# A fused forward and backward pass: spectra stores moved to SyncE, lag matrices made earlier, and a new order of transfers in the last stage

## The chip, the cores and the metric

The kernel runs on one core of a Trainium2 chip. The metric is the device time of one execution in microseconds. Before the change the median of three runs is 741.45 us (740.36 to 741.85). The core has five engines with an instruction order of their own: TensorE (PE: matrix products into PSUM), VectorE (DVE), ScalarE (ACT), GpSimd (POOL) and SyncE (SP, which here only issues transfers). SP, ScalarE and GpSimd can each issue DMA transfers; the issue is an instruction in that engine's order, so whatever stands behind it on that engine waits for it.

## The reference, cut to what matters

With L = 2048 rows, D = 512 channels, N = 128 states and F = 1792 hidden units, all inputs bf16:

```
xn  = layernorm(x)
K   = real(sum_n C * exp(dt*A*l) * dt*B)           # 512 x 2048, a state-space kernel
s   = causal_conv(xn, K) + xn * Dskip               # through a transform of length 2L
h   = xn @ w1;  f = silu(h) @ w2;  g = silu(f)
out = x + s * g
```

The function returns `out` and, for a given grad_out, the gradients of x, of the eight state-space parameters, of w1 (output 10, 512 x 1792) and of w2 (output 11): twelve outputs. The backward pass of the dense part needs dh = (df @ w2^T) * silu'(h), then dx += dh @ w1^T and dw1 = xn^T @ dh.

## The kernel before

The rows stand in 16 tiles of 128. The convolution is done with matrix products against tables of a transform that is split into four classes kt; U, D and K spectra (of xn, of the gradient and of the state-space kernel) are made class by class, multiplied on VectorE (`cplx_mul`), and turned back. Spectra and other large intermediates that do not fit into the on-chip memory go to DRAM and come back (`UXd`, `DXd`, `Kud`, `hTd`, `dhd`, `Sd`, `gd`). There are six stages, one function each, and the order of instructions on each engine is the order in which the Python code issues them: nothing is rescheduled. Generators (`prev`, `fin`, `gx` and so on) are advanced step by step to lay one part's work between the steps of another. Tiles come from pools on two stacks, `k.left` and `k.right`; where a pool is closed and another opened, the new tile lies over the old one, and its first writer waits for the old one's last reader, transfers included.

Each transfer signals one of eight completion semaphores, in turn; SP and ScalarE share one set of eight, in the program's order, and GpSimd has another. So an issue also waits until the transfer eight places earlier in that list has landed.

What the change and the prediction's steps touch:

- **End of stage 2** (`stage_2`, from about L1082). `load_K` (L885 on) brings the state-space kernel K back from DRAM in 17 pieces over all three queues (SP, ScalarE, GpSimd). Then come, on GpSimd's queue, one table (`TFs1`), one spectrum of another class (`UXl`), the store of spectrum `UXd[3]` (inside `radix(3)`) and the store of `DXd[3]` (L1099). `rad_inv` on VectorE writes the tile BK3 (L97, L98) in memory that overlaps the stored U spectrum; `dskip_out` and then the first step of K's transform (`add_eo`, L1174) follow it.
- **Stage 4** (the loop over t0 in steps of 2). At t0 == 10 `gsum_sel` (L1192) makes the lag matrices: 0/1 matrices that later sum parts of a gradient by lag group. It is a few index patterns on GpSimd and 15 short VectorE operations. Stage 5's weight-gradient products (L1595) run on TensorE beside it.
- **Out0** (L1344 on) makes output 0: it loads S, g and x tiles, multiplies and adds on VectorE, stores the result and issues the next three loads. In the last loop of stage 6 it runs at four of the sixteen steps, and its transfers are issued by ScalarE.
- **Stage 6, first loop** (n = 0 to 27). `B.dh(n)` (L1858) does silu'(h) on ScalarE (`sd`, L132), eight matmuls da (L1870), the product dhT on VectorE (L1871), then has SP load h for step n + 3 (`ld_h`, tile `hsb`, three buffers) and store the previous step's dhT (`flush`, L1879). For n < 7 one piece of W1 is loaded with a DMA transpose into W1T behind each step (L1950). From n = 7 on, a generator `B.dx` interleaves half a row tile of dx = dhT @ W1T (seven matmuls, L1893) with each step; it reads the first half of W1T in its first half and the second half in its second. `B.dot` transposes the next 512 rows of the gradient (L1849).
- **Stage 6, last loop** (16 steps of 16 matmuls, L1981). Four column chunks times four row blocks of output 10. For each of them ScalarE copies PSUM into `o10b` (three buffers, L1983). SP loads the chunks `dhc` with DMA transposes (L1946), two ahead of each of the first steps, and stores the o10b of the step before (L1993).

Of the kernel before, what the change touches and what calls it, by code (L numbers as in the profile page):

```python
# [1002 lines left out]
def stage_2(k):  # L1003

    nc = k.nc
    lo, ro = k.left, k.right
    k.tf2 = ro.open("tf2"); k.xs = ro.open("xs", 2); sb = ro.open("sb"); k.slot[1] = (sb, ro.open("cyb")); dsc = ro.open("dsc"); uw = ro.open("uw", 2)
    st = k.st = {}
    k.put = nc.sync.dma_start
    DskT = k.DskT = uw.tile([P, P], BF16, name="DskT", bufs=1)  # L1010
    nc.gpsimd.memset(DskT[:], 0.0)
    gw = gen_w2t(k, lo.open("w2s"))

    def rad(XU):
        t = k.mm.tile([P, 2, 4, W], BF16, name="r4_t", tag="cm_t2")[:].rearrange("p e (c m) w -> p e c m w", c=2)
        rad4(nc, XU[:, :, 0:2], XU[:, :, 2:4], XU, t, False)

    def radix(b, q=nc.gpsimd):
        XU = st[b]["A"]
        rad(XU)  # L1020
        q.dma_start(k.UXd[b], XU[:])

    def front(b):
        st[b] = {}
        TFs = st["TF"] = k.TFs
        k.TFs = ld_tf(k, (b + 1) % 4)
        return fwd_classes(k, uw, k.xn, TFs, st[b])
    for b in range(2):
        fr = front(b)
        if b == 0:  # L1030
            open_tables(k, 1, nc.sync)
            open_y(k, 1)
            ld_tab(k, 1)
            next(gw)
            for e in range(2):
                nc.sync.dma_start(DskT[65 * e:65 * e + 33:32], k.ins["Dskip"].rearrange("(s d) -> s d", d=P)[2 * e:2 * e + 2])
        for _ in fr:
            tables_0(k)
    for b in range(NB):
        Kg = chunk_K(k, b, k.tabs[b])  # L1040
        Tc, Tn = k.gc.get(b + 1), k.gt.get(b + 1)
        gx = gen_xt(k, k.xs, b)
        gy = [gen_yt(k, k.xs, i) for i in (4 * b, 4 * b + 2)]
        sl = [gx] * 11 + [g for g in gy for _ in range(2)]
        if b == 3:
            for _ in Kg:
                pass
            break
        if b == 2:
            sl, gy2 = sl[:11], sl[11:]  # L1050
        if b:
            open_y(k, b + 1)
        fr = front(b + 2) if b < 2 else fwd_classes(k, dsc, k.DS, st["TF"], st.setdefault("D", {}))
        for j in range(15):
            if j in ((3, 9), (0, 3, 6), (0, 3))[b]:
                next(gw)
            if j in ((8, 10, 12, 14), (1, 4, 7, 10), (8, 13))[b]:
                next(fr)
            if j < 4:
                next(Tc, None)  # L1060
            if j == 0 and b < 2:
                next(k.gt[b])
            if j == 4 and b < 2:
                ld_tab(k, b + 2)
            if j % 2 == 0:
                next(Kg, None)
            if j < len(sl):
                next(sl[j])
            if b == 0 and j in (1, 3):
                radix(j // 2)  # L1070
            if b == 2 and j == 3:
                radix(2)
            if j == 10 and b < 2:
                open_tables(k, b + 2, nc.sync)
            if j in (4, 6, 8, 10, 12, 14):
                next(Tn)
    store_K(k)
    next(k.gt[2])
    for g in gy2:
        next(g)  # L1080
    held = []
    k.put = lambda *a: held.append(a)  # L1082
    lo.close("w2s", "xc", "ko", "sa")
    k.do = lo.open("do")
    K_b = k.do.tile([P, T, D], BF16, name="K_b", tag="DO")
    for _ in fr:
        pass
    load_K(k, K_b)
    k.by = lo.open("by"); k.uxp = lo.open("uxl")
    k.TFs1 = ld_tf(k, 1, nc.gpsimd)  # L1090
    UX = ld_ux(k, 0)
    radix(3)
    next(k.gt[3])
    sl = iter(sl)
    for n in range(8):
        next(next(sl))
    XD = st["D"]["A"]
    rad(XD)
    nc.gpsimd.dma_start(k.DXd[3], XD[:])  # L1099
    PX = cplx_mul(nc, k.mm, st[3]["A"], XD, conj_a=True)  # L1100
    ro.close("uw", "dsc", "cyb")
    k.BY = k.by.tile([P, 4, 2, 4, W], BF16, name="BY", tag="B")
    k.tn = lo.open("tn"); bk3 = lo.open("bk3")
    kq = k.kq = lo.open("kq")
    k.sel = lo.open("sel")
    k.row = k.sel.tile([DK, P], BF16, name="row")
    psd = k.psd = k.ps.tile([P, DK, P], F32, name="ps_dsk", tag="pz", bufs=1)
    for kt in range(4):
        for t in range(T):
            nc.tensor.matmul(out=psd[:, kt], lhsT=k.DS[:, t, kt * P:(kt + 1) * P], rhs=k.xn[:, t, kt * P:(kt + 1) * P], start=(t == 0), stop=(t == T - 1))  # L1110
    gk = gen_kt(k, kq, K_b, UX)
    next(gk)
    k.BK3 = rad_inv(k, bk3, "BK3", PX)
    k.dskb = dskip_out(k)
    return gk, sl, held


# [226 lines left out]
class Out0:  # L1344
# [15 lines left out]
    def run(self, t0, pool=False):  # L1360
        k, (S, g, x) = self.k, self.ins.pop(t0)
        TT = k.nc.vector.tensor_tensor
        TT(out=S[:], in0=S[:], in1=g[:], op=ALU.mult)
        TT(out=S[:], in0=S[:], in1=x[:], op=ALU.add)
        q = k.nc.gpsimd if pool else k.nc.scalar
        q.dma_start(k.o0_v[:, t0:t0 + TS, :], S[:])
        self.load(t0 + 2 * TS, q)

# [46 lines left out]
def stage_4(k):  # L1415

    nc = k.nc
    lo, ro = k.left, k.right
    y = k.y
    k.TI = {}  # L1420
    k.bk = lo.open("bk")
    dx = DXform(k, k.bk, k.kq)
    for kt in range(2):
        for _ in dx.front(kt):
            pass
    dx.mul(0)
    dx.inv(0)
    for t0 in range(0, T, TS):
        if t0 == 4:
            dx.mul(1)  # L1430
            dx.inv(1)
        if t0 == 8:
            for _ in dx.front(2):
                pass
            dx.mul(2)
        if t0 >= 4:
            y.sil(t0)
            y.pre(t0)
        TI = y.TI.pop(t0)
        ps = k.pd.tile([P, TS, W], F32, name="ps_v", tag="pd")  # L1440
        inv_mm(k, ps, [k.BY[:, i] for i in range(4)], TI, t0, (0, 1, 2, 3))
        S_s = k.y2.tile([P, TS, W], BF16, name="S_s", tag="S_s")
        nc.scalar.activation(out=S_s[:], in_=ps[:], func=ACT.Copy, scale=1.0 / L)  # L1443
        if t0 + 6 < T:
            y.load_ti(t0 + 6)
        else:
            k.TI[t0 + 6 - T] = ld_ti(k, k.tip, t0 + 6 - T)
        o = y.out(t0, S_s)
        if 2 <= t0 < T - 4:
            y.load(t0 + 4)  # L1450
        nc.sync.dma_start(*o)
        if t0 == 6:
            store_rows(k, k.row, k.outs[9], k.dskb)
        if t0 == 10:
            dx.inv(2)
            k.sels = gsum_sel(k, k.sel)
            k.pr.mul(0)
            k.pr.load(1)
        if t0 + 4 == T:
            k.w2 = Dw2(k)  # L1460
    ro.close("y2")
# [372 lines left out]
class Bwd:  # L1834
# [23 lines left out]
    def dh(self, n):  # L1858
        k, nc = self.k, self.k.nc
# [10 lines left out]
                nc.tensor.matmul(out=ps[:, j], lhsT=self.W2T[:, ft // 2, dk, j * P:(j + 1) * P], rhs=self.DOT[tc_][:, dk], start=(dk == 0), stop=(dk == DK - 1))  # L1870
        nc.vector.tensor_tensor(out=self.dhT[:, f0:f0 + 2, :], in0=ps[:], in1=sd[:], op=ALU.mult)  # L1871
        if n + 3 < 28:
            self.ld_h(n + 3)
        self.flush()
        self.pend.append((k.dhd[tc_, f0 * P:(f0 + 2) * P].rearrange("(a p) t -> p a t", p=P), self.dhT[:, f0:f0 + 2, :]))

# [47 lines left out]
def stage_6(k):  # L1924
    nc = k.nc
    lo, ro = k.left, k.right
    fw = k.fw
    W1T = k.tfp.tile([P, FT, D], BF16, name="W1T", tag="W1")
# [13 lines left out]
    def ld_ch(i, tc_):  # L1942
# [2 lines left out]
            ch[i] = pool.tile([P, T, FC], BF16, name="dhc", tag=tag)  # L1945
        nc.sync.dma_start_transpose(ch[i][:, 4 * tc_:4 * tc_ + 4, :], k.dhd[tc_, FC * i:FC * i + FC])  # L1946
    for n in range(28):
        B.dh(n)
        if n < 7:
            nc.sync.dma_start_transpose(W1T[:, 2 * n:2 * n + 2], k.ins["w1"][:, 256 * n:256 * n + 256])  # L1950
        next(prev, None)
        if n == 8 or n >= 21:
            next(fin, None)
        if n in (22, 23, 24, 26):
            ld_ch(0, min(n - 22, 3))
        if n in (8, 9):
            z.load((n - 8) * TS, nc.sync)
        if n in (11, 14, 16, 18):
            z.run(TS * (11, 14, 16, 18).index(n), True)
        if n % 7 == 5 and n < 26:  # L1960
            B.dot(n // 7 + 1)
        if n % 7 == 6:
            for _ in prev:
                pass
            prev = B.dx(n // 7, B.dhT)
# [1 line left out]
    order = [(i, tc_) for i in (1, 2, 3) for tc_ in range(4)]  # L1967
    ld_ch(*order.pop(0))
    ld_ch(*order.pop(0))
    pend = []  # L1970
    at = (6, 8, 10, 12)
    next(prev)
    for i in range(4):
        for dk in range(DK):
# [6 lines left out]
                nc.tensor.matmul(out=ps[:], lhsT=k.xn[:, t, dk * P:(dk + 1) * P], rhs=ch[i][:, t, :], start=(t == 0), stop=(t == T - 1))  # L1981
            ob = ww.tile([P, FC], BF16, name="o10b", tag="o10b")
            nc.scalar.copy(out=ob[:], in_=ps[:])  # L1983
            next(prev, None)
            next(fin, None)
            it = DK * i + dk
# [2 lines left out]
            if i == 1 and dk == 0:  # L1989
                B.rest()  # L1990
                B.flush()
            if pend:
                nc.sync.dma_start(*pend.pop())  # L1993
            pend.append((o10v[:, dk, FC * i:FC * i + FC], ob[:]))
    assert next(fin, k) is k
    nc.sync.dma_start(*pend.pop())
    ro.close("fp4", "ww", "fx", "fw", "wt", "tip", "tf2", "tfp")
    lo.close("oz", "fb", "do", "mm", "ds")

# [29 lines left out]
```

## Time and profile before

| | |
|---|---|
| median of 3 runs | 741.45 us |
| the profiled execution: device time | 748.97 us |
| its span, first to last instruction | 747.2 us |
| mean granted TensorE clock | 0.957 |
| busy: TensorE | 659.1 us (88%) |
| busy: VectorE | 619.4 us (83%) |
| busy: ScalarE | 418.1 us (56%) |
| busy: GpSimd | 122.4 us (16%) |
| DRAM traffic | 253 GB/s over the span |

The profile is one execution, so every duration in it belongs to 748.97 us and not to the median. "Busy" counts an engine's instructions and not the DMA issues. Times in windows and timelines count from the first instruction. "Idle before" is the time in which an engine did nothing ahead of an instruction, and the arrow names what was released last; where it says "issue" the profile saw no releaser, which can be a transfer. The granted clock is the share of TensorE's full rate: at 0.5 a matmul takes twice as long.

### The profile page before, as it was taken

How to read it: one execution, taken by the hardware profiler on the slowest of the kernel's cores; microseconds unless marked ns; L12 is line 12 of the kernel's file. 1: busy time of each engine (PE TensorE's matmuls, PEld its weight loads, DVE VectorE, ACT ScalarE, POOL GpSimd, SP SyncE). 2: the span in 40 equal slices, each digit the busy share in tenths (PEclk: the TensorE clock that was granted, in tenths of full speed). 3: DMA queues.
4: the chain of work that ended last, by engine and by line, in shares of the span. 5: the costliest groups of instructions: out<-in, count | busy, mean ns of one | idle time of the engine just before them, and what ended most of it. 6: DMA issues, size and time to landing. Idle time of an engine off the chain costs nothing. (4 is left out here: it accounts for less than half of the span.)

```text
span 747.2 us, 13309 instructions
## 1 busy us (share of the span) xinstructions
PE 659.1 (88%) x5132; PEld 336.8 (45%) x5132; DVE 619.4 (83%) x965; ACT 418.1 (56%) x513; POOL 122.4 (16%) x184
## 2 busy tenths in 40 slices
PE   4778877799878777999999899999999979999988
PEld 2434444354545656554444344444444434444543
DVE  6799999989899799599999999944577549899570
ACT  4789888995568967365534322344656523443231
POOL 2334171021011002100001212041222002200000
PEclk9998998899999998999999999999999989999999
DMA  9647767889898978999767879799886997999992
GB/s 268 236 165 246 236 229 240 266 298 358 268 317 275 301 222 182 296 347 359 287 227 286 287 288 353 215 316 335 272 283 232 240 307 248 321 242 221 225 266 87
DMA packets 167361, 198.83 MB, mean 266 GB/s; under 512 B 58461, under 2 KB 128484, under 8 KB 161378
## 3 DMA queue, kind: packets, MB, share of 16 engines
q1 hardware_dynamic: 150882, 132.63, 58.1%
q0 software_dynamic: 11200, 51.98, 19.8%
q10 hardware_dynamic: 5216, 13.38, 5.4%
q8 instruction: 40, 0.66, 0.4%
q14 instruction: 23, 0.19, 0.1%
HBM read 105.38 MB, written 83.38 MB: 253 GB/s over the span
## 5 line engine op out<-in xcount | busy, mean ns | idle before, releaser
L607 PE MATMUL ps_h<-XNT,W 128*128 128x512 bf16 x224 | 60.8, 421 | 12.2 <-ACT hs L610 12.2
L1188 PEld LDWEIGHTS <-TIs 128*128 128x128 bf16 x384 | 37.7, 99 | 51.7 <-issue 4.9
L1893 PE MATMUL ps_dx<-W1T,dhT 128*128 128x512 bf16 x224 | 53.8, 384 | 5.5 <-DMA W1T<-in_B_w_dram 4.6
L580 PE MATMUL ps_o<-W,aT 128*128 128x512 bf16 x224 | 55.7, 399 | 2.5 <-DVE ak L76 2.5
L1870 PE MATMUL ps_da<-DOT,W2T 128*128 128x512 bf16 x224 | 53.9, 388 | 2.3 <-DVE dhT L1871 2.3
L1981 PE MATMUL ps_w<-dhc,xn 128*128 128x448 bf16 x256 | 51.3, 361 | 3.1 <-ACT o10b L1983 3.1
L1595 PE MATMUL ps_w<-DO_all,AW 128*128 128x512 bf16 x224 | 52.0, 380 | 0.0
L1871 DVE TENSOR_TENSOR dhT<-ps_da,sd 128x1024 bf16<-128x1024 f32 x28 | 34.1, 1222 | 18.9 <-ACT sd L132 14.0
L1902 ACT ACTIVATE dxn<-dxn,c,rstd 128x512 f32<-128x512 f32 x16 | 13.0, 814 | 65.6 <-DVE c L1901 65.6
L1781 DVE TENSOR_TENSOR T<-Vb,YTl 128x2048 bf16<-128x2048 bf16 x16 | 19.6, 1224 | 35.2 <-ACT Vb L1772 34.9
L1164 PEld LDWEIGHTS <-TFs 128*128 128x128 bf16 x312 | 30.1, 98 | 38.6 <-issue 2.1
L934 ACT COPY XT<-pt_xt 128x1024 bf16<-128x1024 bf16 (+1 forms) x44 | 41.4, 1009 | 5.2 <-DMA XTd<-XT 3.2
L1772 ACT CAST Vb<-ps_V 128x1024 bf16<-128x1024 f32 x32 | 31.7, 1013 | 16.8 <-PE ps_V L1770 11.5
L1164 PE MATMUL ps_f<-K_b,TFs 128*128 128x512 bf16 x168 | 39.1, 379 | 1.5 <-DMA K_b<-Kud 1.3
L607 PEld LDWEIGHTS <-W 128*128 128x128 bf16 x224 | 22.8, 106 | 38.3 <-issue 21.8
L1981 PEld LDWEIGHTS <-xn 128*128 128x128 bf16 x256 | 25.5, 100 | 28.1 <-issue 5.6
L580 PEld LDWEIGHTS <-aT 128*128 128x128 bf16 x224 | 22.9, 102 | 32.0 <-issue 8.3
L1893 PEld LDWEIGHTS <-dhT 128*128 128x128 bf16 x224 | 22.0, 99 | 33.3 <-issue 7.5
L1870 PEld LDWEIGHTS <-W2T 128*128 128x128 bf16 x224 | 22.0, 99 | 30.2 <-issue 6.4
L998 PE MATMUL ps_f<-xn,TFs 128*128 128x512 bf16 x128 | 32.7, 411 | 3.3 <-DMA TFs<-TFd 3.3
L1164 PE MATMUL ps_f<-DS,TFs 128*128 128x512 bf16 x144 | 33.0, 379 | 1.8 <-ACT S_s L1443 1.8
L932 PE MATMUL pt_xt<-ident_bfloat,X 128*128 128x128 bf16 x328 | 25.7, 228 | 8.9 <-ACT XT L934 6.9
(342 smaller groups left out, 1510.6 us busy)
## 6 DMA issues: line engine op xcount, KB each, us to landing
TIs<-TId SPq DMA_DIRECT2D x24, 512.0 KB, 6.6
XTd<-XT SPq DMA_DIRECT2D x20, 512.0 KB, 5.8
XTl<-XTd SPq DMA_DIRECT2D x15, 512.0 KB, 8.6
hTd<-hs SPq DMA_DIRECT2D x28, 256.0 KB, 3.5
akd<-ak SPq DMA_DIRECT2D x28, 256.0 KB, 3.3
UXl<-UXd POOLq DMA_DIRECT2D x7, 1024.0 KB, 7.7
dhd<-dhT SPq DMA_DIRECT2D x28, 256.0 KB, 4.2
XYd<-XYg SPq DMA_DIRECT2D x25, 256.0 KB, 4.0
```

Source lines behind the costliest of these rows:

```text
L580: nc.tensor.matmul(out=pso[:], lhsT=aT[:, ft, tt * P:(tt + 1) * P], rhs=W2[:, ft, :], start=(ft == 0), stop=(ft == FT - 1))
L607: nc.tensor.matmul(out=ps[:, j], lhsT=W1[:, dk, ft * P:(ft + 1) * P], rhs=XNT[:, dk], start=(dk == 0), stop=(dk == DK - 1))
L934: nc.scalar.copy(out=XT[:, j0:j0 + len(ks)], in_=pt[:, 0:len(ks)])
L998: nc.tensor.matmul(out=ps[:, c, :], lhsT=TFs[:, t1 + 4 * j, c, :], rhs=src[:, t1 + 4 * j, :], start=(j == 0), stop=(j == 3))
L1164: nc.tensor.matmul(out=ps[:, c, :], lhsT=tab(j), rhs=at(t1 + 4 * j), start=(n == 0), stop=(n == 4 * len(terms) - 1))
L1188: nc.tensor.matmul(out=ps[:, j, :], lhsT=TIs[:, j, 2 * kt + c, :], rhs=B[kt][:, c, (t0 + j) % 4, :], start=(kt == 0 and c == 0), stop=(kt ...
L1595: nc.tensor.matmul(out=ps[:], lhsT=A[:, t, :], rhs=k.DO[:, t, :], start=(t == 0), stop=(t == T - 1))
L1772: nc.scalar.copy(out=self.V[i][:, g2], in_=ps[:].rearrange("p b c n -> p c b n"))
L1870: nc.tensor.matmul(out=ps[:, j], lhsT=self.W2T[:, ft // 2, dk, j * P:(j + 1) * P], rhs=self.DOT[tc_][:, dk], start=(dk == 0), stop=(dk == ...
L1871: nc.vector.tensor_tensor(out=self.dhT[:, f0:f0 + 2, :], in0=ps[:], in1=sd[:], op=ALU.mult)
L1893: nc.tensor.matmul(out=psx[:], lhsT=dhT[:, ft, t % 4 * P:(t % 4 + 1) * P], rhs=self.W1T[:, ft, :], start=(ft == 0), stop=(ft == FT - 1))
L1981: nc.tensor.matmul(out=ps[:], lhsT=k.xn[:, t, dk * P:(dk + 1) * P], rhs=ch[i][:, t, :], start=(t == 0), stop=(t == T - 1))
```

## The change

Six edits. (1) The stores of UXd[3] and DXd[3] are issued by SP instead of GpSimd. (2) `gsum_sel` is called at the end of stage 2, behind `dskip_out`, instead of in stage 4. (3) Out0's transfers in the last loop are issued by SP instead of ScalarE, and it runs one step later. (4) The h loads issued in steps 0 to 6 are ScalarE's. (5) The W1T pieces are issued ahead of steps 0 to 5, two of them ahead of step 0, instead of behind steps 0 to 6. (6) Each o10b block is stored by ScalarE directly behind its copy instead of by SP one step later.

```diff
@@ stage_2
-    radix(3)
+    radix(3, nc.sync)
...
-    nc.gpsimd.dma_start(k.DXd[3], XD[:])
+    nc.sync.dma_start(k.DXd[3], XD[:])
...
     k.BK3 = rad_inv(k, bk3, "BK3", PX)
     k.dskb = dskip_out(k)
+    k.sels = gsum_sel(k, k.sel)
     return gk, sl, held
@@ Out0.run
-        q = k.nc.gpsimd if pool else k.nc.scalar
+        q = k.nc.gpsimd if pool else k.nc.sync
@@ stage 4, t0 == 10
             dx.inv(2)
-            k.sels = gsum_sel(k, k.sel)
             k.pr.mul(0)
             k.pr.load(1)
@@ dh
-            self.ld_h(n + 3)
+            self.ld_h(n + 3, nc.scalar if n < 7 else None)
@@ stage_6, first loop
     for n in range(28):
+        for m in ((0, 1), (2,), (3,), (4,), (5,), (6,))[n] if n < 6 else ():
+            nc.sync.dma_start_transpose(W1T[:, 2 * m:2 * m + 2], k.ins["w1"][:, 256 * m:256 * m + 256])
         B.dh(n)
-        if n < 7:
-            nc.sync.dma_start_transpose(W1T[:, 2 * n:2 * n + 2], k.ins["w1"][:, 256 * n:256 * n + 256])
@@ stage_6, last loop
-    pend = []
-    at = (6, 8, 10, 12)
+    at = (7, 9, 11, 13)
...
             nc.scalar.copy(out=ob[:], in_=ps[:])
+            nc.scalar.dma_start(o10v[:, dk, FC * i:FC * i + FC], ob[:])
...
-            if pend:
-                nc.sync.dma_start(*pend.pop())
-            pend.append((o10v[:, dk, FC * i:FC * i + FC], ob[:]))
     assert next(fin, k) is k
-    nc.sync.dma_start(*pend.pop())
```

## The prediction

> **What bounds the kernel.** I read the shares first (TensorE busy 88% of the 747.2 us span, VectorE 83%), then TensorE's timeline for its idle time, then the waits and the queue timelines of the three places that the diff touches. The diff leaves TensorE's instructions and VectorE's number of them as they are, so it can win only TensorE's idle time and its half clock. The profiled execution took 748.97 us, 1.8 us of them outside the span, and lies 7.5 us above the median of the runs, 741.45; I work in its rows and carry the sum over at the end.
>
> Waits of 578 to 612 us (start of the last stage): total us, times, longest.
> ```profile
> ACT sd L132 <- DMA hsb<-hTd: 6.8, 5, 1.8
> PE ps_dx L1893 <- DMA W1T<-in_B_w_dram: 4.6, 2, 3.4
> ```
> Timeline of SP and then of TensorE there (start, length, instruction, idle time before it):
> ```profile
> 589.06 0.39 SPq L1879 DMA_DIRECT2D dhd<-dhT  x1
> 589.50 1.43 SPq L1950 DMA_TRANSPOSE W1T<-in_B_w_dram  x1
> 591.02 0.75 SPq L1856 DMA_DIRECT2D hsb<-hTd  x1
> 591.87 0.39 SPq L1879 DMA_DIRECT2D dhd<-dhT  x1
> 592.31 1.60 SPq L1950 DMA_TRANSPOSE W1T<-in_B_w_dram  x1
> ```
> ```profile
> 603.28 1.01 PE L1893 MATMUL ps_dx<-W1T,dhT 128*128 128x512 bf16 x2 [3.44 <-DMA W1T<-in_B_w_dram]
> 604.08 3.62 PE L1870 MATMUL ps_da<-DOT,W2T 128*128 128x512 bf16 x8
> 609.63 1.89 PE L1870 MATMUL ps_da<-DOT,W2T 128*128 128x512 bf16 x8
> ```
> SP issues one step's three transfers in about 2.8 us (589.50 to 592.31; 2.4 to 2.8 over the seven steps), and the seventh W1T transpose goes out only at 597.67. TensorE needs W1T whole for dx, waits 1.18 and 3.44 us, and then eight matmuls take 3.62 us instead of 1.89: half clock (the windows give 0.50 for 604 to 608 us).
>
> Waits of 696 to 747 us, then SP, then TensorE:
> ```profile
> ACT o10b L1983 <- DMA out_dram<-o10b: 17.3, 5, 5.2
> PE ps_w L1981 <- ACT o10b L1983: 3.1, 2, 2.7
> ```
> ```profile
> 702.08 3.78 SPq L1946 DMA_TRANSPOSE dhc<-dhd  x2
> 705.91 0.58 SPq L1993 DMA_DIRECT2D out_dram<-o10b  x1
> ```
> ```profile
> 714.39 3.19 PE L1981 MATMUL ps_w<-dhc,xn 128*128 128x448 bf16 x16 [0.45 <-ACT o10b L1983]
> 720.27 13.95 PE L1981 MATMUL ps_w<-dhc,xn 128*128 128x448 bf16 x64 [2.69 <-ACT o10b L1983]
> ```
> Stores of the gradient blocks stand behind pairs of dhc transposes on SP, ScalarE's copies wait for the buffers, TensorE for the copies.
>
> At the end of stage 2, VectorE, and later TensorE:
> ```profile
> 304.04 0.41 DVE L96 TENSOR_TENSOR r_t<-cm_t 128x512 bf16<-128x512 bf16 x1
> 312.78 1.22 DVE L97 TENSOR_TENSOR BK<-r_t 128x2048 bf16<-128x2048 bf16 x1 [8.32 <-issue]
> ```
> ```profile
> 395.80 4.48 PE L1164 MATMUL ps_f<-DS,TFs 128*128 128x512 bf16 x20 [1.78 <-ACT S_s L1443]
> 426.62 1.02 PE L1188 MATMUL ps_v<-BK,TIs 128*128 128x512 bf16 x4 [3.03 <-ACT S_s L1443]
> ```
> The 8.32 us idle end when the store of UXd[3] has landed (issued by POOL at 301.79, 10.9 us to landing, so 312.7): BK3 lies over the buffer it reads.
>
> **Part 1, W1T and h (last stage's start).** Without a stall, TensorE's work from 578.14 to da(10) is 10 da of 1.73, 3 half dx of 1.51 and the DOT transposes, about 1.0: 22.8 us, so da(10) could start at 600.9 instead of 609.63. At stake: 8.7 us. In the changed order SP issues two transposes before dh(0), then one ahead of each step, at 1.45 us each (mean of the seven). The buffer comes free about 579.3 (last AW copy ends 577.41, store landing 1.7). Transposes: 579.3 and 580.75, then 582.2, 584.05 and, held by completion (below), 585.95, 588.6, 590.5; the last is issued by 592.0 and, with the measured landing of 5.2, lands at 595.7. That is before dx needs the second half of W1T (after da(7) and da(8)).
> The seven h loads go to ScalarE, 0.35 to 0.53 each as its store issues show, 3.5 us in all. SP and ScalarE share eight completion semaphores in turn, in program order: an issue waits until the transfer eight places earlier has landed. With landing 5.2 the h loads of steps 5 to 8 then leave at 584.5, 587.4, 589.3 and 591.2, and the sd behind each in ScalarE's order waits too. A step costs ScalarE 1.06 (sd) + 0.5 (issue) = 1.55, below TensorE's 1.73. With h landing in 3.7 us, da(7) starts at 592.7, da(8) 595.9, da(9) 599.1, da(10) 602.35. Against 609.63: 7.3 us. The new wait is ScalarE's, on a transpose's landing L: roughly da(10) = 591.8 + 2L, so another microsecond of landing costs 2. L was 4.7 to 5.8 in seven cases, alone in the queue; back to back I allow 6.5. I take **-6.5**; bounds -8.7 (no stall) and -4 (L = 6.9). From 610 to 680 us TensorE is busy nearly throughout (idle 0.64, 0.31, 1.26), so the gain passes on.
> The Trainium skill ("Trainium Kernel Development and Optimization", Key Constraints) says that issuing from several engines saves only the sequencer's issue time, as all share 16 DMA engines. By that alone the h move would bring nothing where DMA engines bind; here SP's issue time of 2.8 us against 1.73 is itself the limit, so I count it.
>
> **Part 2, the tail.** Each out10 block leaves ScalarE right behind its copy, so no store stands behind SP's 3.7 us transpose pairs. The out0 stores and reloads go to SP, 16 stores and 7 h loads away from it. Added on ScalarE: 16 issues of about 0.4, beside copies of 0.53 every 3.0 to 3.1 us: covered, ScalarE being 23% to 36% busy there. The completion order adds waits: stores 2 to 4 wait for transposes and stores issued 5 to 8 us earlier, 5 to 8 for O and ob stores, 13 to 15 for z loads; each comes, in the compiled program's order of transfers, no later than about the next copy. TensorE has three PSUM buffers, a margin of 2 to 3 us. What goes: 0.45 + 2.69 idle, half clock after it (64 matmuls in 13.95 against 64 x 0.19 = 12.1, so 1.8) and a gap of 0.15 at 734.2: 5.1. What ends last is still the last copy and its store (3.6 us after the last matmul now). **-5.0**; bounds -5.3, and -3 if one stall of about 1 us and its half clock stay.
> By the Trainium skill ("TensorE: Matmul & The Clock Gate", Part 1) the clock halves after an idle window of about 3.4 us; the 2.69 us stall is shorter and still cost half clock, so the row decides. By the page the 1.8 us would not be won and the sum be 1.8 smaller.
>
> **Part 3, spectra and lag matrices.** Taken from POOL: two 1 MB issues. On SP, UXd[3] stands behind the K pieces, its issue held until an earlier piece has landed (the 512 KB one issued at 289.06, whose landing I put at 297 from the 13.1 us and 384 KB of its neighbour, less its head start; TensorE uses K at 301.35 at the latest). K loads fill the DMA engines (share 1.01 at 109 GB/s around 295 us), so UXd cannot land much before they end, and it now shares the engines with TFs1 and UXl, which were ahead of it on POOL (each 1 MB, landing 5.6 and 8.1). I put its landing t at 305 to 309, middle 307, instead of 312.7.
> The lag matrices are 5.38 us of VectorE (429.05 to 434.43). They move from a stretch where TensorE runs on without VectorE (428.04 to 482) to one where VectorE is about 98% busy (316 to 428) and TensorE twice waits for it through S_s (1.78 and 3.03, shown above). So they cost in the new place what the earlier landing gives: add_eo(0) starts at t + 2.46 (BK) + 1.41 (dskip) + 5.38 = t + 9.25, against 316.65, and not before 314.47, when its PSUM copy is there. At 307 that is 316.25: 0.4 gained. Ends: +2.2 (t below 305.2) and -1.6 (t = 309). With half clock after 423.6 kept or lost, -2.2 to +2. Where K lands 1 to 2 us later by the stores, the 1.78 absorbs it. I take **0**.
>
> **Sum**: -6.5 - 5.0 + 0 = -11.5 on 748.97, so 737.5 for an execution like the profiled one; times 741.45/748.97 gives 730.1. Some stalls may be smaller in the runs, which are 1% faster: I say 731.0.
>
> **Rivals.**
> - Both last-stage stalls go and the front is neutral: 731 (728 to 734). Chance 0.57.
> - The front gives 2 to 4 more, the spectra landing early and the stall at 423.6 with its half clock gone: 727. For it: 8.3 us idle is there to win. Against: the sels eat 5.4. Chance 0.09.
> - The front costs 2 to 4: UXd, sharing with TFs1 and UXl, lands at 312 again and the sels come on top (5.4 late less what idle of VectorE remains): 734.5. Chance 0.09.
> - The first stall moves to ScalarE (L = 7.5: da(10) at 606.8, 2.8 won): 735. Chance 0.10.
> - The tail keeps most of its stall, ScalarE held by transposes' landings: 735.5. Chance 0.07.
> - Slower: seven transposes back to back with stores and h between land late. It decides in one place, ScalarE's h issues: from L = 8.9 da(10) is later than 609.63, and from L = 12.2 (2 x 12.2 - 17.8 = 6.6) it takes away the tail's 5.0 and 1.5 more. At L = 13 da(10) is at 617.8: 8.2 - 5.0 = 3.2 slower, 744.6. Against it: 4.7 to 5.8 measured, 5.3 with transposes in pairs (dhc). Chance 0.04.
> - The parts cancel within 0.2% (about 1.5 us, what a measurement of this kernel tells from no change; its runs spread by 1.5): 741. Chance 0.04.
>
> The range, 726 to 738, leaves out the last two and the outer part of the front's cases. Faster 0.92, same 0.04, slower 0.04.
>
> **What would show it.** Right: no TensorE wait on W1T, no granted clock of 0.50 in the last stage's first 30 us, da(10) about 7 us earlier from the stage's start; ScalarE held on h issues instead; o10b copies 0.1 us behind their matmuls, no stall and no half clock near 720; the 8.3 us before BK L97 shortened by some 5 and followed by the sels; TensorE's wait near 426 within 2 us of 3.03. Wrong: W1T landings above 7 us, TensorE waiting for sd or o10b, K_b waits above 1.34 near 303 us, or a longer wait near 395 and 426.

## The result

The changed kernel takes 740.87 us (median of 22 runs) beside 745.74 for the kernel before in as many runs: a ratio of **0.9943, interval 0.9921 to 0.9965**. Two later sets gave 0.9887 (0.985 to 0.9923, only five runs) and 0.9931 (0.990 to 0.9961). So it is faster, by 0.6% or a little more, where 1.4% was forecast. The ratios and intervals here leave out executions in a slower state and are not quotients of these medians (740.87/745.74 is 0.9935), and the traces of two runs below that were taken in that state, at a granted clock of 0.84 (the tail alone and the first repeat of the changed kernel), are not read. The three runs shown before the prediction (741.45) were among the lower ones of the kernel before: 4.3 us of the 9.9 between 731.0 and 740.87 are theirs.

Both kernels issue the same 5132 matmul rows in one order, so the two traces can be laid on each other by TensorE's landmarks (us; da(n) stands for the da matmuls of step n):

| stretch on TensorE | before | changed | difference |
|---|---|---|---|
| start to the second product with K (end of stage 2; the first stands ahead of a wait for K) | 303.07 | 299.13 | -3.94 |
| from there to da(0), start of the last stage | 275.07 | 275.94 | +0.87 |
| da(0) to da(10) | 31.49 | 31.37 | **-0.12** |
| da(10) to the first of the last 221 matmuls | 86.43 | 86.44 | +0.01 |
| from there to the last matmul | 47.14 | 42.00 | **-5.14** |

The profiled executions differ by 8.5 us of span (747.2 and 738.7). Nearly half of it lies ahead of the first instruction that was moved: the traces of the kernel before and of the start alone (two runs below), the same code up to there, reach the first landmark between 298.09 and 303.07 us. The second row holds what edits 1 and 2 do, but it takes 274.1 to 280.5 us in the twelve traces that are read, whatever the edits, so this one pair says nothing about them. In the last three rows the tail won what was forecast, the start of the last stage nothing.

The tail, TensorE's timeline in the changed kernel:
```profile
695.47 30.43 PE L1980 MATMUL ps_w<-dhc,xn 128*128 128x448 bf16 x160
725.83 0.22 PE L985 MATMUL pt_row<-ident_bfloat,ob 128*4 128x128 bf16 x1
725.98 9.25 PE L1980 MATMUL ps_w<-dhc,xn 128*128 128x448 bf16 x48
```
160 matmuls run without a gap in 30.43 us; the 2.69 us stall and the half clock behind it are gone.

Waits from 692 us on:
```profile
ACT o10b L1982 <- PE ps_w L1980: 16.8, 9, 2.7
...
ACT o10b L1982 <- DMA out_dram<-O: 5.1, 1, 5.1
```
ScalarE now mostly waits for TensorE, as it should. Once it still stands for 5.1 us in front of a copy: its own store is held until a store of O, behind SP's transposes, has landed. TensorE, with three PSUM buffers, runs on through it. Edits 3 and 6 were not tried apart, so which of the two won how much of the 5.14 us stays open.

The start of the last stage, waits of 575 to 607 us:
```profile
DVE dhT L1871 <- ACT sd L132: 14.6, 7, 3.6
...
ACT sd L132 <- DMA W1T<-in_B_w_dram: 4.8, 2, 3.7
...
ACT sd L132 <- DMA hsb<-hTd: 3.9, 3, 2.0
PE ps_da L1870 <- DVE dhT L1871: 3.5, 3, 2.0
ACT DOT L1850 <- DMA W1T<-in_B_w_dram: 2.8, 1, 2.8
```
TensorE's wait on W1T is no longer there. In its place ScalarE waits for W1T pieces (4.8 and 2.8: its h issue is held until one has landed, and sd or DOT stands behind the issue), and for h. TensorE's timeline shows what comes of it:
```profile
590.36 1.89 PE L1870 MATMUL ps_da<-DOT,W2T 128*128 128x512 bf16 x8 [2.02 <-DVE dhT L1871]
595.04 3.13 PE L1870 MATMUL ps_da<-DOT,W2T 128*128 128x512 bf16 x8 [2.79 <-ACT DOT L1850]
```
The half clock came back too (eight matmuls in 3.13 us instead of 1.89). SP's issues (SPq in the rows), in the same stretch:
```profile
576.13 5.72 SPq L1949 DMA_TRANSPOSE W1T<-in_B_w_dram  x3
581.95 0.53 SPq L1879 DMA_DIRECT2D dhd<-dhT  x1
582.52 1.90 SPq L1949 DMA_TRANSPOSE W1T<-in_B_w_dram  x1
584.47 0.58 SPq L1879 DMA_DIRECT2D dhd<-dhT  x1
585.09 3.60 SPq L1949 DMA_TRANSPOSE W1T<-in_B_w_dram  x1
```
A transpose's issue, 1.45 us in the old order, took up to 3.60 here, and the one landing that the profile could match took 6.5 us, not 5.2.

### The profile page after: what moved, and what is told of

The parts are those of the page before. It is cut to its first block, busy times and chain, and to the rows that moved or that the text cites. A ratio compares the mean times of both kernels' runs of the same rounds, so it can differ in the third digit from the quotient of the medians.

```text
span 738.7 us, 13319 instructions
## 1 busy us (share of the span) xinstructions
PE 655.2 (89%) x5132; PEld 336.4 (46%) x5132; DVE 619.3 (84%) x965; ACT 418.5 (57%) x513; POOL 121.2 (16%) x182
## 5 line engine op out<-in xcount | busy, mean ns | idle before, releaser
L580 PE MATMUL ps_o<-W,aT 128*128 128x512 bf16 x224 | 53.6, 388 | 2.4 <-DVE ak L76 2.4
L1980 PE MATMUL ps_w<-dhc,xn 128*128 128x448 bf16 x256 | 49.3, 352 | 0.0
L1980 PEld LDWEIGHTS <-xn 128*128 128x128 bf16 x256 | 25.0, 98 | 23.5
L1189 PE MATMUL ps_v<-BK,TIs 128*128 128x512 bf16 x128 | 31.7, 406 | 3.2 <-ACT S_s L1444 3.2
```

The costliest lines, as they stand in the source:

```text
L580: nc.tensor.matmul(out=pso[:], lhsT=aT[:, ft, tt * P:(tt + 1) * P], rhs=W2[:, ft, :], start=(ft == 0), stop=(ft == FT - 1))
L1189: nc.tensor.matmul(out=ps[:, j, :], lhsT=TIs[:, j, 2 * kt + c, :], rhs=B[kt][:, c, (t0 + j) % 4, :], start=(kt == 0 and c == 0), stop=(kt ...
```

## The experiments

**Theory A**: the tail is the whole gain. **Theory B**: the start gains its 6.5 in most executions, and something else gives it back. First the parts one by one.

*The tail alone* (edits 3 and 6; the rest as before).

> The kernel before with edits 3 and 6 alone (out10 blocks stored by ScalarE behind their copies, Out0's transfers on SyncE one step later). Theory A (the tail is the whole gain: between the two traces TensorE's last 240 matmuls gained 5.1 us, and nothing else that was changed gained): 5.1 of 746, ratio 0.993. Theory B (the start of the last stage gains 6.5 as forecast, in most executions, and another part gives it back): 0.993 here too. A ratio above 0.997 would speak against both.

Measured: 0.9927 (0.9903 to 0.9951).

*The front alone* (edits 1 and 2).

> The kernel before with edits 1 and 2 alone (spectra stored by SyncE, lag matrices made at the end of stage 2). Theory A: 0.999 to 1.001; in the trace of the changed kernel the spectrum lands some 6 us earlier and the lag matrices take 5.4 of it. Theory B: this is the part that gives back, 1.005 to 1.009.

Measured: 0.9984 (0.9957 to 1.0011): not told apart from nothing, and no loss that could hide 6.5 us.

*The start alone* (edits 4 and 5).

> The kernel before with edits 4 and 5 alone (h loads of steps 0 to 6 issued by ScalarE, W1T pieces ahead of the steps). Theory A: 0.999 to 1.002: TensorE's wait on W1T goes and a wait of about the same length on ScalarE, held at its h issues until a W1T piece has landed, takes its place. Theory B: 0.991 (6.5 of 746).

Measured: 0.9944 (0.992 to 0.9969), against A, and less than B; but its trace has 30.46 us from da(0) to da(10), no gain.

*Without the start* (the changed kernel without edits 4 and 5).

> The changed kernel without edits 4 and 5: h on SyncE and W1T pieces behind each step, as before. Theory A: the same as the changed kernel, 0.993 to 0.995. Theory B: slower than the changed kernel by 6.5 us, 1.002 to 1.004.

Measured: 0.9906 (0.9874 to 0.9939), against B: without edits 4 and 5 the kernel was no slower. The two ratios contradict each other if both are taken at their word, so both were repeated, with one more kernel that asks why.

*The changed kernel, and the start alone, again.*

> The changed kernel as it is, beside the three below. So far: 0.9943 of the kernel before, and 0.9906 for the same without edits 4 and 5. Theory A2 (edits 4 and 5 cost about 1 to 2 us: the stretch from da(0) to da(10) took 31.4 us in the changed kernel's trace, and 28.6 and 29.5 in two executions of the old order; the 31.5 of the first trace was a long one): 0.993 to 0.995, da(0) to da(10) again 30 to 32 us. Theory B (they gain 6.5): 0.984 to 0.987.

Measured: 0.9887 (0.985 to 0.9923), from five runs: outside both forecasts, between them.

> The kernel before with edits 4 and 5 alone, once more, as its first ratio of 0.9944 stands against its own trace (30.5 us from da(0) to da(10), not shorter than the old order). Theory A2: 1.000 to 1.003. Theory B: 0.991 to 0.993.

Measured: 0.9975 (0.9945 to 1.0005), again between the two; da(0) to da(10) 28.90 us.

*h on GpSimd's queue.* This separates two reasons for the lost gain: ScalarE held in its order (A-order), or full DMA engines (A-engines).

```diff
-            self.ld_h(n + 3, nc.scalar if n < 7 else None)
+            self.ld_h(n + 3, nc.gpsimd if n < 7 else None)
```

> The changed kernel with the h loads of steps 0 to 6 on GpSimd's queue, which has completion semaphores of its own, so that no h issue waits for a W1T piece and ScalarE issues none. Theory A-order (ScalarE, held in order at its h issues, is what keeps the start long): da(0) to da(10) in 24 to 26 us, ratio 0.986 to 0.988. Theory A-engines (the 16 DMA engines, full from the second W1T piece on, keep it long, whoever issues): 29 to 32 us, 0.993 to 0.995.

Measured: 0.9909 (0.9873 to 0.9944), da(0) to da(10) 30.98 us. The stretch is as A-engines has it; the ratio lies between the two forecasts and does not tell them apart. GpSimd's, ScalarE's and TensorE's timelines, a line each:
```profile
577.79 0.54 POOL L1856 DMA_DIRECT2D hsb<-hTd  x1 [1.81 <-ACT sd L132]
```
```profile
586.25 2.00 ACT L132 ACTIVATE sd<-hsb 128x1024 bf16<-128x1024 bf16 x2 [6.40 <-DMA hsb<-hTd]
```
```profile
588.61 3.57 PE L1870 MATMUL ps_da<-DOT,W2T 128*128 128x512 bf16 x8 [4.47 <-DVE dhT L1871]
```
The h load of step 3 is issued at 577.79, early, and waits for no W1T piece. sd of step 3 still waits for it until 586.25, 8 us later. Nothing in any engine's order holds it; it lies in the DMA engines beside the transposes. The windows (PE, PEld, DVE, ACT, POOL busy, granted clock, DMA share, GB/s) say the same:
```profile
578.00:582.00 4.00, 3.26 (x16) 1.46 (x15) 3.08 (x3) 1.50 (x2) 1.40 (x3) 1.00 1.17 148
582.00:586.00 4.00, 2.15 (x10) 0.88 (x9) 0.02 (x1) 0.00 (x0) 0.00 (x0) 1.00 0.98 130
```
The 16 DMA engines are busy all the time (1.17, 0.98) and move only 130 to 148 GB/s. That is A-engines. How much of the 8 us is GpSimd's own queue was not tried: the three h loads that it issued earlier in this trace, ahead of the transposes, took 4.8 to 6.6 us to land.

*W1T earlier.* If the engines are full in this stretch, the pieces belong in another one. W1T lies over the ring that holds the column blocks of the previous product, and each third of it is free as soon as its last block has been read. This kernel is the changed one without edits 4 and 5. `k.W1T` is a view of that ring, `ld_w1t` the transpose of one piece; the first hunk below the view is in stage 5's loop over column blocks, the last in stage 6, where h stays on SyncE.

```diff
-    W1T = k.tfp.tile([P, FT, D], BF16, name="W1T", tag="W1")
+    W1T = k.W1T
...
+        if ft > 10:
+            for m in ((4, 5), (0, 1), (2, 3))[ft - 11]:
+                ld_w1t(k, m)
...
+        if n == 1:
+            ld_w1t(k, 6)
         B.dh(n)
```

> The changed kernel without edits 4 and 5, and with six of the seven W1T pieces loaded at the end of stage 5 instead, each as soon as the part of the buffer below it has been read (pieces 4 and 5 behind the 12th column block of output 11, 0 and 1 behind the 13th, 2 and 3 behind the 14th); in the traces the DMA engines are idle there for some 8 us. h stays on SyncE. Theory A-engines and A-order alike: da(0) to da(10) in 23 to 25 us, 0.983 to 0.986 of the kernel before. If stage 5's own transfers are held up by the pieces instead: about 0.991.

Measured: 0.9913 (0.9877 to 0.9949); da(0) to da(10) 25.37 us in its trace, near what was expected, but the ratio is that of the case in which stage 5's transfers are held up. Its profiled execution was also its fastest run (733.76 us, the median 741.92), so one trace does not show where the others lost the gain. SP's timeline does not settle it:
```profile
558.64 9.73 SPq L1579 DMA_TRANSPOSE AW<-in_B_w_dram  x2
568.47 0.68 SPq L1607 DMA_DIRECT2D out_dram<-AW  x1
```
Two pieces stand for 9.73 us on SP, ahead of a store of stage 5. But in the changed kernel SP stands at the same place for 14.25 us with three such stores, which wait for ScalarE's copies. Where the gain went stays open.

The next four runs repeat the pair that decides between A and B, take the transposes' cost away, and move the pieces to a place where the DMA engines were idle.

> The changed kernel, once more beside the next two, as its ratio came out 0.9943 and 0.9887. Theory A-engines (edits 4 and 5 move nothing; the tail is nearly the whole gain): 0.990 to 0.994, and no more than 0.3% from the same kernel without them. da(0) to da(10) 30 to 31.5 us.

Measured: 0.9931 (0.990 to 0.9961); 30.47 us from da(0) to da(10).

> The changed kernel without edits 4 and 5, once more. Theory A-engines: within 0.3% of the changed kernel, da(0) to da(10) 28.5 to 31 us. Theory B (edits 4 and 5 gain 6.5): 0.9% slower than the changed kernel.

Measured: 0.9952 (0.9918 to 0.9985); 30.81 us. It is within 0.3% of the changed kernel, and the two intervals leave no room for B's 0.9%: B is out. The start alone (0.9944 and 0.9975) and this pair still leave open a gain of a few tenths of a per cent by edits 4 and 5; no trace shows where it would be.

*Plain loads in place of the transposes.*

```diff
-            nc.sync.dma_start_transpose(W1T[:, 2 * m:2 * m + 2], k.ins["w1"][:, 256 * m:256 * m + 256])
+            nc.sync.dma_start(W1T[:, 2 * m:2 * m + 2], k.ins["w1"][0:128, 128 * m:128 * m + 1024].rearrange("p (a d) -> p a d", a=2))
```

> The changed kernel with each W1T piece loaded by a plain transfer of the same size and place instead of a DMA transpose; W1 is then not transposed, so output 1 is computed from other numbers. Same issues, queues and order, but packets of 2 KB in place of 256 bytes, which took 23 ns each in the traces (1024 a piece: 1.5 us of all 16 engines). Theory A-engines: the engine time of the pieces falls from some 10 us to 3 to 4, da(0) to da(10) in 24 to 27 us, 5 us off the changed kernel's time. If the stretch were bound by DRAM bandwidth or by the number of issues: 29 to 31 us, no change.

Measured: 0.9858 (0.9807 to 0.991), and 23.86 us from da(0) to da(10). Its SP and its windows:
```profile
577.94 1.37 SPq L1949 DMA_DIRECT2D W1T<-in_B_w_dram  x3
581.24 0.39 SPq L1879 DMA_DIRECT2D dhd<-dhT  x1
581.67 0.47 SPq L1949 DMA_DIRECT2D W1T<-in_B_w_dram  x1
```
```profile
581.00:585.00 4.00, 3.74 (x18) 1.73 (x18) 2.68 (x4) 2.53 (x3) 0.00 (x0) 1.00 1.03 361
585.00:589.00 4.00, 4.00 (x31) 2.23 (x30) 2.43 (x2) 1.54 (x2) 0.00 (x0) 1.00 1.05 377
```
The same bytes by the same queues in the same order, the engines as full (1.03), but 361 to 377 GB/s through them, and TensorE nearly without a gap. So neither DRAM nor the count of issues set the limit. Two things went with the transposes, their time in the DMA engines and their longer issues on SP (three in 5.72 us in the changed kernel, in 1.37 here). This run alone does not part them; the run with h on GpSimd's queue does, as the h load there stood behind no issue of SP's and TensorE waited for no W1T piece. What is left, as far as these runs go, is the transposes' time in the DMA engines.

*W1T earlier, second place.* As the first early kernel, but with four pieces behind the 13th block, three behind steps 0 to 2, and four h buffers (the lines for the buffers are not shown).

```diff
+        if ft == 12:
+            for m in (4, 5, 0, 1):
+                ld_w1t(k, m)
...
         B.dh(n)
+        if n < 3:
+            ld_w1t(k, (2, 3, 6)[n])
```

> The changed kernel without edits 4 and 5, with W1T pieces 4, 5, 0 and 1 loaded behind the 13th column block of output 11 (later than in the run before, when stage 5's own loads are done), 2, 3 and 6 behind steps 0 to 2, and a fourth h buffer, loaded ahead with the other three. Theory A-engines: da(0) to da(10) in 24 to 26 us, 0.983 to 0.987 of the kernel before; and less time than the first early version if that one's pieces held up stage 5. If it comes out as the changed kernel although the stretch is 5 us shorter in the trace, the gain is lost in stretches that the profile's one execution doesn't show.

Measured: **0.9804 (0.9751 to 0.9857)**, 23.60 us from da(0) to da(10), from five runs. It beats both kernels, and by more than was forecast. SP and TensorE:
```profile
572.12 5.82 SPq L1579 DMA_TRANSPOSE AW<-in_B_w_dram  x4
578.08 0.48 SPq L1607 DMA_DIRECT2D out_dram<-AW  x1
582.02 0.33 SPq L1864 DMA_DIRECT2D hsb<-hTd  x1
```
```profile
583.30 7.07 PE L1878 MATMUL ps_da<-DOT,W2T 128*128 128x512 bf16 x32 [0.74 <-DVE dhT L1879]
590.21 1.06 PE L1857 MATMUL pt_do<-ident_bfloat,DO_all 128*128 128x128 bf16 x16
591.10 3.62 PE L1878 MATMUL ps_da<-DOT,W2T 128*128 128x512 bf16 x16
594.55 1.67 PE L1901 MATMUL ps_dx<-AW,dhT 128*128 128x512 bf16 x7
```
Four transposes go out before da(0), at 578.93, and TensorE then runs into dx with one wait of 0.74: the 22.8 us that the prediction added up for this stretch without a stall, and that wait, make 23.5. The windows of the second run without edits 4 and 5 show the hole that they fill:
```profile
568.00:572.00 4.00, 4.00 (x72) 2.10 (x64) 1.62 (x3) 2.31 (x3) 0.00 (x0) 1.00 0.21 80
572.00:576.00 4.00, 4.00 (x40) 1.75 (x37) 2.86 (x4) 2.21 (x3) 0.00 (x0) 1.00 0.10 33
576.00:580.00 4.00, 3.70 (x21) 1.39 (x20) 2.00 (x3) 2.09 (x3) 0.56 (x1) 1.00 0.10 33
```
From 568 us to 580 us (da(0) is at 578.38) the DMA engines were 10% to 21% busy. Which of early_2's two edits (the place, the fourth buffer) gave how much was not tried apart.

## Why the prediction was right or wrong

**Part 1, wrong.** The step that failed is the bound: "SP's issue time of 2.8 us against 1.73 is itself the limit, so I count it." SP was busy, but it was not what the work waited for: the 16 DMA engines were full. From da(0) to da(10) the old order took 31.49, 28.63, 29.48 and 30.81 us in four traces, the changed one 31.37, 30.46, 28.90 and 30.47: means of 30.1 and 30.3, no difference that their spread could show. Over this stretch the DMA share is 1.01 in the trace before and 1.06 in the changed one. The profile before had it already, in windows that the prediction did not weigh; two of them, and then one of the changed kernel:
```profile
588.00:596.00 8.00, 7.97 (x50) 3.94 (x48) 4.22 (x4) 3.58 (x4) 0.00 (x0) 1.00 1.16 279
600.00:604.00 4.00, 0.72 (x2) 0.25 (x2) 0.07 (x1) 0.00 (x0) 0.00 (x0) 0.74 1.03 196
```
```profile
582.00:586.00 4.00, 3.21 (x16) 1.37 (x15) 1.88 (x2) 1.06 (x1) 0.00 (x0) 1.00 1.27 208
```
The pieces' 7168 packets of 256 bytes took 22.8 ns each in the changed kernel's records: 10.2 us of all 16 engines, beside h, dhd and the next loads. In none of these runs did another issuing engine or another order take this time away. The old order paid it as a wait on W1T, the new one on h and on ScalarE's held issues.

The terms built on it failed with it. On the time axis of the trace before (da(0) comes 3.07 us earlier in the changed one) the first three transposes left as forecast; the last four were put at 584.05, 585.95, 588.6 and 590.5 and left at 585.6, 588.2, 592.4 and 594.7, and the last landing, put at 595.7, came at 601.2. The h loads of steps 5 to 8 left 0.6, 3.2, 3.4 and 5.5 us late. The landing taken as 5.2 was that of pieces spread by SP, and the trace before matches three of them, not seven; sent back to back, the one that is matched took 6.5 and the issues up to 3.60. By the prediction's own 591.8 + 2L a landing of 6.5 would have left 4.8 us of gain, so the landing alone does not explain the miss. The cadence of 1.55 us on ScalarE counted its own work, though the prediction itself had the hold (an h issue behind a W1T landing) and a rival for it. That rival (735, chance 0.10) named the wait that the trace then showed, but it too left 2.8 us of gain, and GpSimd's queue showed that removing the hold gives nothing.

The Trainium skill ("Trainium Kernel Development and Optimization", Key Constraints) says that issuing from several engines only saves the sequencer's issue time, as all queues share the 16 DMA engines. The prediction cited it and set it aside. The runs agree with it: h from SP, ScalarE and GpSimd gave 28.6 to 31.5 us alike.

**Part 2, right.** 5.0 forecast; 47.14 to 42.00 is 5.14. All eight traces read of kernels with the new tail have 42.00, the four with the old one 46.29 to 47.72. The forecast that ScalarE's stores would be held "no later than about the next copy" was too kind: ScalarE stood 5.1 us at one of them. The copy behind it came at 716.41, where an even spacing of 3.03 us after the copy at 710.80 gives 713.8: about 2.6 us late, within the margin of 2 to 3 us that the prediction gave the three PSUM buffers.

**Part 3, right.** 0 forecast; 0.9984 with an interval on both sides of 1, some 4 us wide, as are the forecast's own bounds. VectorE in the changed kernel:
```profile
303.19 1.22 DVE L97 TENSOR_TENSOR BK<-r_t 128x2048 bf16<-128x2048 bf16 x1 [1.23 <-DMA UXd<-XU]
...
307.06 0.17 DVE L1198 CAST vb<-lvf 128x16 bf16<-128x16 f32 x1
...
312.45 0.69 DVE L1175 TENSOR_TENSOR r_t<-BY 128x1024 bf16<-128x1024 bf16 x1
```
The idle time ahead of BK fell from 8.32 to 1.23, and the lag matrices fill it: 307.06 to 312.45. With the 3.94 us by which this execution was early, BK starts at 307.1 on the time axis of the trace before (forecast: the store lands at 307) and the next step at 316.4 (forecast 316.25, before 316.65). TensorE's wait near 422 is 3.19, before 3.03 plus 0.41. From the second product with K to the first matmul of `ps_g` behind this wait TensorE takes 132.58 us before (303.07 to 435.65) and 133.04 changed (299.13 to 432.17): 0.5 us lost in this pair, inside the bounds.

**The sum.** With Part 1 at 0 it would have been -5 us, a ratio of 0.993 of 745.74, beside the measured 0.9943, 0.9887 and 0.9931. The absolute number suffered besides from a median of three runs.

## What to carry to other kernels

Before a stall is put down to a queue's issue time, look at the DMA share in the same window: at a share of 1 and a low rate in GB/s, small packets (here DMA transposes) fill the engines, and neither another queue nor another order helps. Look instead for a stretch where the share is near zero, and whether the destination is free by then. One trace of each kernel is not enough where executions differ by 1%: a stretch between two landmarks on TensorE, read from several traces, told within 1.5 us what the ratios left open.

## What the runs showed that was not expected

The granted clock fell after shorter idle times than one would read from the 3.44 us case: after 2.69 us in the tail before, after 2.79 us in the changed kernel, and in the second run of the changed kernel without edits 4 and 5 after less still (TensorE, then two windows):
```profile
600.63 0.59 PE L1893 MATMUL ps_dx<-W1T,dhT 128*128 128x512 bf16 x2 [1.78 <-DMA W1T<-in_B_w_dram]
603.01 1.01 PE L1893 MATMUL ps_dx<-W1T,dhT 128*128 128x512 bf16 x2 [1.79 <-DMA W1T<-in_B_w_dram]
603.82 3.62 PE L1870 MATMUL ps_da<-DOT,W2T 128*128 128x512 bf16 x8
```
```profile
600.00:602.00 2.00, 0.59 (x2) 0.19 (x2) 0.74 (x1) 0.00 (x0) 0.00 (x0) 0.82 1.06 298
602.00:604.00 2.00, 0.99 (x3) 0.40 (x3) 0.00 (x0) 0.00 (x0) 0.00 (x0) 0.50 1.13 381
```
The granted clock of 0.82 over the first window puts the fall near 601.3 us: behind the wait of 1.78 us, and before the second wait had passed. The matmuls behind them ran at half clock. In another execution (the front alone) waits of 1.80 and 1.83 us left it whole. The Trainium skill ("TensorE: Matmul & The Clock Gate", Part 1) gives one idle window of about 3.4 us, free-running; here a wait of 1.78 us went ahead of the fall once, and one of 1.80 us did not bring it. What decides between the two stays open.
